# Loads of k, r and v that wait for the landing of the load two ahead

## The chip, the cores and the metric

The kernel runs on one core of a Trainium2 chip. The metric is device time in microseconds; the lower, the better. The kernel before took 514.64 us, the median of nine runs (513.17 to 515.85).

## What is computed

Two steps follow each other. The first is a recurrence over 768 positions, for 4 batches and 8 heads of 48 channels, in float32:

```python
for t in range(S):
    kt, vt, rt = (k[:, :, t], v[:, :, t], r[:, :, t])
    cur = np.einsum('bhd,bhe->bhde', u[None] * kt, vt)
    y[:, :, t] = np.einsum('bhd,bhde->bhe', rt, state + cur)
    state = w[None, :, :, None] * state + np.einsum('bhd,bhe->bhde', kt, vt)
```

The second is a multiplicative feed-forward net on the 3072 rows of 384 channels which that gives:

```python
a = x @ w1
b = x @ w2
h = a * b @ w3
return (h @ w_out)
```

The weights w1, w2 (384 x 1024), w3 (1024 x 1024) and w_out (1024 x 384) come as float64.

## The kernel before

**The recurrence** is cut into 24 units: 6 chunks of 128 positions (`NCH`), times 4 batches. A unit `n` needs its k and r (in `krin[n % 3]`) and its v (in `vnat[n % 3]`). Each of these three is one DMA of 192 KB, 128 positions by 8 heads by 48 channels, which `load` issues on SP's queue (L197 to L204). In memory a position of one head is a run of 48 numbers, so such a load consists of 1024 runs of 192 bytes.

DVE then scales k and r (`scale`, L392) and forms the products for the diagonal (`rk`, L401; `rku`, L404; `dots`, L408). PE turns k and r (L439) and ACT copies them back (L446, L449). For later units DVE turns blocks itself (`turn_blocks`, L461), SP writes them to a scratch in HBM (`turn_out`, L465) and reads them back in four pieces (`turn_places`, L473), and ACT copies the keys out (`turn_rows`, L478). PE forms the products of the recurrence: `adds` (L505, needs v and the scaled k), `products` (L512, needs the turned k and r), `with_state` (L612, needs the state that ACT spread out in L537), `with_pairs` (L626, needs v). ACT takes the result out as `xT` (`take`, L634).

**The weights** come in 32 pieces, also on SP's queue (`fetch`, L218 to L223): 8 of 768 KB (w1 and w2), 8 of 384 KB (w_out), 16 of 512 KB (w3), into three buffers in turn. Each float64 word is made into a float32 in five steps, two on ACT (`magnitude` L342, `low` L354) and three on DVE (`sign` L347, `high` L350, `total` L357). w3 and w_out are multiplied into one matrix first (`fold`, L370 to L383).

**The net** then runs by chunk: `product_ab` (L652) on PE makes a or b for 128 of the 1024 channels, three matmul steps over 384 channels, into one of two PSUM buffers (`psF`). `take_a` (L658) on ACT copies a out and so frees its buffer, `multiply` (L663) on DVE multiplies b by it and frees the other. The product with the folded matrix is done in seven half-size products (`product` L709, `gather`, `store` L742).

**What sets the order.** For the decay values of this input, the arm with a list of instructions written out by hand is taken: `ORDER` (L22 to L88), whose words are run one after the other by `listed` (L745 to L756). Under `manual_schedule` each of PE, ACT, DVE and SP does its instructions in the order of that list. `kr.4` is the load of k and r of unit 4, `v.4` that of v, `W.4` the fetch of weight piece 4, `y.5` and `z.5` the scratch write and its four reads, `l.11` the ACT copy after them, `M.3` the first ACT step of weight piece 3, `a.1.5.2`, `c.1.5.2`, `b.1.5.2`, `u.1.5.2` are `product_ab` of a, `take_a`, `product_ab` of b and `multiply` for chunk 1, channel block 5. All DMAs of the kernel are issued by SP, in that one order. What stands ahead of the list (the loads of units 0 and 1, weight pieces 0 and 1, w and u, L227 to L237) is placed by the scheduler. The DMAs use eight completion semaphores in turn, so that a DMA is not issued before the eighth one ahead of it has landed.

Of the kernel before, what the change touches and what calls it, by code (L numbers as in the profile page):

```python
# [14 lines left out]
COPY = mybir.ActivationFunctionType.Copy  # L15
ABS = mybir.ActivationFunctionType.Abs
PSUM = bass.MemoryType.PSUM
PE, ACT, DVE, SP = (getattr(mybir.EngineType, x) for x in ("PE", "Activation", "DVE", "SP"))


# [64 lines left out]
u.5.7.2 s.5.3.0 P.5.0.1 s.5.3.2 E.5.1.0 s.5.3.1 s.5.3.3 P.5.0.2 E.5.0.1 P.5.0.3 E.5.0.2 P.5.0.4 E.5.0.3 P.5.0.5  # L85
E.5.0.4 P.5.0.6 E.5.0.6 E.5.0.5 D.5.0.0 P.5.1.2 E.5.0.7 D.5.0.1 P.5.1.1 E.5.1.2 P.5.1.3 E.5.1.1 P.5.1.4 E.5.1.3
P.5.1.5 E.5.1.4 P.5.1.6 E.5.1.6 E.5.1.5 D.5.1.0 E.5.1.7 D.5.1.1
"""  # L88


@with_exitstack
def kernel(
# [34 lines left out]
    nc = tc.nc  # L127
# [66 lines left out]
    units = [(c, b) for c in range(NCH) for b in range(B)]  # L194
    NU = len(units)

    def load(n, which="krv"):  # L197
        if n >= NU:
            return
        c, b = units[n]  # L200
        ts = slice(c * C, (c + 1) * C)
        for nm, src, dst in (("k", k, krin[n % NIN][:, 0]), ("r", r, krin[n % NIN][:, 1]), ("v", v, vnat[n % NV][:, :, :D])):
            if nm in which:
                nc.sync.dma_start(out=dst, in_=src[b, :, ts, :].rearrange("h t d -> t h d"))  # L204

    w1 = const.tile([P, DF // STRIP, KM, STRIP], F32)
    w2 = const.tile([P, DF // STRIP, KM, STRIP], F32)
# [6 lines left out]
    pieces = [src for src, _ in strips] + [moe_w_out[j * P:(j + 1) * P, None, :] for j in range(KF)] \  # L214
        + [moe_w3[j * P:(j + 1) * P, None, z * PIECE:(z + 1) * PIECE] for j in range(KF) for z in range(NW3)]
    landed = {}
# [11 lines left out]
    for i in range(2):  # L228
        nc.sync.dma_start(out=wucol[i * PAD:i * PAD + D], in_=w.rearrange("(p i) (d o) -> i d p o", i=2, o=1)[i])
    load(0, "kr")  # L230
    fetch(0)
    nc.sync.dma_start(out=ub.rearrange("t h d -> t (h d)"),
                      in_=u.rearrange("h d -> (h d)").rearrange("(o n) -> o n", o=1).to_broadcast([P, DM]))
    load(0, "v")
    load(1, "kr")
    fetch(1)
    load(1, "v")  # L237
# [10 lines left out]
    pn_in = const.tile([C, 2, H, PAD], F32)  # L248
    with tc.tile_pool(name="once", bufs=1) as once, tc.tile_pool(name="psW", bufs=2, space=PSUM) as psW:

# [29 lines left out]
    def program(fast):  # L280
        with ExitStack() as arm:
            body(arm, fast)

    def body(arm, fast):
# [4 lines left out]
        once = fold_pool.enter_context(tc.tile_pool(name="fold", bufs=1))  # L289
        psT = arm.enter_context(tc.tile_pool(name="psT", bufs=2, space=PSUM))  # L290
        psA = arm.enter_context(tc.tile_pool(name="psA", bufs=1, space=PSUM))
        psY = arm.enter_context(tc.tile_pool(name="psY", bufs=1, space=PSUM))
        psF = arm.enter_context(tc.tile_pool(name="psF", bufs=2, space=PSUM))

# [532 lines left out]
            seven(NCH - 2)  # L827
            seven(NCH - 1)

        at_start = dict(landed)  # L830
        (listed if fast else plain)()
        landed.clear()
        landed.update(at_start)

# [34 lines left out]
```

## Time and profile before

| | |
|---|---|
| median of nine runs | 514.64 us (513.17 to 515.85) |
| the profiled execution: its own time | 514.53 us |
| its span, first instruction to last | 512.7 us |
| PE busy (matmul) | 489.8 us, 96% of the span |
| DVE busy | 278.2 us, 54% |
| ACT busy | 183.1 us, 36% |
| moved by DMA | 52.72 MB; 77729 of 96865 packets under 512 B |
| loads of k, r, v: number, median from issue to landing | 24 each; 3.9, 4.4, 4.1 us |
| weight pieces of 768, 512, 384 KB: the same | 8, 16, 8; 6.2, 5.1, 3.6 us |
| mean granted TensorE clock | 0.996 |

All times of the profile are of one execution. A line of the page or the timeline gives start and length, engine, source line, what is written and read, and in brackets how long the engine stood idle before it and what ended that. "SPq" is the issue of a DMA: its length is the time that SP spends in issuing, not that of the transfer. The landing of a transfer is told apart from it, as the time from issue to landing. "issue" as the cause of idle time means that the engine waited for nothing that the profile shows.

### The profile page before, as it was taken

The page shows a single profiled execution, that of the slowest core. Times are in us where ns is not written, and L with a number is a line of the kernel's source. Part 1 is how long each engine was busy: PE and PEld are TensorE (multiplying, and loading weights), DVE is VectorE, ACT ScalarE, POOL GpSimd, SP SyncE. Part 2 cuts the span into 40 slices and gives each one's busy share as a digit, 9 for nine tenths or more (in the row PEclk, how much of TensorE's full clock was granted, in tenths as well). Part 3 has the DMA queues.
Part 4 walks back from the last instruction along what each step waited for, and adds up shares of the span by engine and source line. Part 5 has one row for each costly group of instructions (what it writes and reads, how often), then busy time and mean ns, then how long its engine had stood idle before and what let it go on. Part 6 is the DMA issues. An engine that isn't in the chain of part 4 may idle for free.

```text
span 512.7 us, 12195 instructions
## 1 busy us (share of the span) xinstructions
PE 489.8 (96%) x5192; PEld 320.9 (63%) x5192; DVE 278.2 (54%) x587; ACT 183.1 (36%) x455; POOL 6.0 (1%) x23
## 2 busy tenths in 40 slices
PE   1789999999999999999999999999999999999996
PEld 1667555455466666678887487564965654855486
DVE  6978998888386866756325432285322215221442
ACT  3767556666377754403103200341061410001000
POOL 4000000000000000000000000000000000000000
PEclk9989999999999999999999999999999999999999
DMA  7998797768549770304402201230050100000001
GB/s 170 232 249 221 184 246 194 190 226 238 148 118 224 191 205 15 78 1 101 132 32 77 64 0 46 64 110 2 1 163 9 49 1 0 17 15 17 1 17 67
DMA packets 96865, 52.72 MB, mean 103 GB/s; under 512 B 77729, under 2 KB 88226, under 8 KB 96802
## 3 DMA queue, kind: packets, MB, share of 16 engines
q1 hardware_dynamic: 96802, 51.86, 37.5%
q8 instruction: 43, 0.70, 0.6%
q14 instruction: 20, 0.16, 0.1%
HBM read 39.65 MB, written 12.19 MB: 101 GB/s over the span
## 4 chain that ended last, share of the span: by engine, by line
PE 86%; DMA 6%; DVE 4%; issue 2%; ACT 1%; SPq 1%; DVEq 0%; ACTq 0%
PE ps_a L652 22%; PE ps_b L652 22%; PE ps_w L380 8%; PE ps_y L612 3%; PE ps_s4b L709 3%; PE ps_a12b L709 3%; PE ps_a22t L709 3%; PE ps_s2t L709 3%; PE ps_s3t L709 3%; PE ps_s1t L709 3%; PE ps_y L626 3%; PE ps_a11b L709 3%; PE ps_a L512 2%; DMA tt<-scratch 2%; PE ps_a L505 2%
## 5 line engine op out<-in xcount | busy, mean ns | idle before, releaser
L652 PE MATMUL ps_a<-xT,w 128*128 128x512 f32 (+1 forms) x300 | 132.5, 585 | 0.0
L652 PE MATMUL ps_b<-xT,w 128*128 128x512 f32 (+1 forms) x300 | 131.0, 578 | 0.0
L652 PEld LDWEIGHTS ps_b<-xT,w 128*128 128x128 f32 x300 | 56.0, 190 | 62.4 <-issue 56.9
L663 DVE TENSOR_TENSOR abt<-ps_b,a 128x512 f32<-128x512 f32 (+1 forms) x50 | 33.4, 667 | 110.4 <-PE ps_b L652 110.4
L652 PEld LDWEIGHTS ps_a<-xT,w 128*128 128x128 f32 x300 | 56.1, 193 | 57.1 <-issue 53.5
L658 ACT COPY a<-ps_a 128x512 f32<-128x512 f32 (+1 forms) x50 | 28.1, 565 | 130.2 <-PE ps_a L652 126.4
L537 ACT COPY wide<-st 64x192 f32<-64x192 f32 x88 | 30.6, 348 | 58.9 <-DVE st L529 28.1
L380 PE MATMUL ps_w<-wo,w3T 128*128 128x384 f32 x128 | 42.5, 487 | 0.0
L419 ACT ACTIVATE AT<-same,dg 128x64 f32<-128x64 f32 x160 | 40.4, 336 | 5.4 <-DVE dg L408 2.9
L380 PEld LDWEIGHTS ps_w<-wo,w3T 128*128 128x128 f32 x128 | 23.9, 190 | 15.7 <-ACT wide L537 0.2
L354 ACT ACTIVATE t<-raw 128x512 uint32<-128x512 uint32 (+2 forms) x32 | 22.4, 706 | 7.8 <-DVE w3n L350 5.0
L626 PE MATMUL ps_y<-AT,vnat 64*64 64x64 f32 x1152 | 22.7, 222 | 0.6 <-issue 0.6
L392 DVE TENSOR_TENSOR krs<-krin,pn_in 128x768 f32<-128x768 f32 x24 | 22.8, 950 | 0.5 <-PE ps_a L505 0.4
L540 DVE COPY_PREDICATED AT<-later,ps_a 128x512 f32<-128x512 int32 x24 | 17.5, 730 | 9.5 <-PE ps_a L505 5.8
L612 PEld LDWEIGHTS ps_y<-tt,wide 128*32 128x32 f32 x1056 | 15.9, 110 | 10.6 <-issue 6.3
L505 PE MATMUL ps_a<-vnat,krs 64*64 64x48 f32 x704 | 16.8, 224 | 5.6 <-DVE krs L392 3.3
L626 PEld LDWEIGHTS ps_y<-AT,vnat 64*64 64x64 f32 x1152 | 19.3, 134 | 3.9 <-issue 2.0
L612 PE MATMUL ps_y<-tt,wide 128*32 128x64 f32 x1056 | 19.7, 221 | 1.7 <-ACT xT L634 1.7
L461 DVE STREAM_TRANSPOSE tr<-krs 128x768 f32<-128x768 f32 x19 | 18.5, 974 | 5.1 <-DMA scratch<-tr 5.0
L505 PEld LDWEIGHTS ps_a<-vnat,krs 64*64 64x64 f32 x704 | 14.3, 139 | 9.7 <-issue 9.2
L512 PEld LDWEIGHTS ps_a<-tt,kT 64*64 64x64 f32 x768 | 14.4, 136 | 7.6 <-issue 3.5
L528 DVE TENSOR_TENSOR st<-ps_a,st 128x192 f32<-128x192 f32 x40 | 14.0, 349 | 8.1 <-PE ps_a L505 4.8
(102 smaller groups left out, 560.4 us busy)
## 6 DMA issues: line engine op xcount, KB each, us to landing
raw<-in_moe_w_dram SPq DMA_DIRECT2D x16, 512.0 KB, 5.1
scratch<-tr SPq DMA_DIRECT2D x19, 384.0 KB, 3.7
raw<-in_moe_w_dram SPq DMA_DIRECT2D x8, 768.0 KB, 6.2
tt<-scratch SPq DMA_DIRECT2D x38, 128.0 KB, 3.1
krin<-in_k_dram SPq DMA_DIRECT2D x24, 192.0 KB, 3.9
krin<-in_r_dram SPq DMA_DIRECT2D x24, 192.0 KB, 4.4
vnat<-in_v_dram SPq DMA_DIRECT2D x24, 192.0 KB, 4.1
raw<-in_moe_w_out_dram SPq DMA_DIRECT2D x8, 384.0 KB, 3.6
```

The lines of the kernel that those rows point to most:

```text
L380: nc.tensor.matmul(ps, lhsT=w3T[j][:, kc, :], rhs=wo[kc], start=(kc == 0), stop=(kc == KF - 1))
L392: nc.vector.tensor_mul(krs[n % NS][:, :, :, :D], kr, pn[:, :, :, :D])
L419: nc.scalar.activation(out=AT[n][:, i, p, :], in_=same, func=COPY, scale=dg[n][:, h:h + 1])
L505: nc.tensor.matmul(added(n)[rows(i), a, p, :], lhsT=kk[rows(a), 2 * p + i, :], rhs=vnat[n % NV][rows(a), 2 * p + i, 0:D], start=True, stop ...
L512: nc.tensor.matmul(upper(n)[rows(a), i, p, :], lhsT=kT[n][rows(i), p, rows(a)], rhs=rT[n][rows(i), p, 2 * a:2 * a + 2], start=True, stop=True)
L537: nc.scalar.copy(out=wide[a][n % 2][rows(i), :, i * D:(i + 1) * D], in_=st[units[n][1]][rows(i)])
L612: nc.tensor.matmul(yt[n][g * Q:(g + 1) * Q, a, q, :], lhsT=wide[a][n % 2][:, p, j * Q:(j + 1) * Q], rhs=rw[:, p, 2 * a:2 * a + 2] if fast ...
L626: nc.tensor.matmul(yt[n][rows(g), a, q, :], lhsT=vv[rows(a), x:x + PAD], rhs=AT[n][rows(a), h % 2, h // 2, :], start=(a, g) not in seen, s ...
L652: nc.tensor.matmul(ps, lhsT=(w1 if x == "a" else w2)[:, z, q, js], rhs=xT[c][:, q, ts], start=(q == 0), stop=(q == KM - 1))
L658: nc.scalar.copy(out=a, in_=ps)
L663: nc.vector.tensor_mul(abt[c, j][:, parts_of_tokens[part]], factor["b", c, j, part], factor["sa", c, j, part])
L709: nc.tensor.matmul(ps, lhsT=of[:, m * C:(m + 1) * C], rhs=w34[:, KH * (x == 1) + j, :DH] if x < 2 else made[b][:, j, :], start=(j == 0), s ...
```

## The change

Every load of k, r or v, from the third on, gets a dependence on the load of k, r or v two ahead of it in the order of the program: it is issued only when that one has landed. Weights, scratch writes and reads, and the stores of the output get none. A list `small` keeps the loads, and is set back for the second arm of the program.

```diff
+ONE_AFTER_THE_OTHER = mybir.DependencyInfo(mybir.DependencyClass.Sync, mybir.DependencyReason.DATA)
...
+    small = []
+
     def load(n, which="krv"):
+
         if n >= NU:
             return
...
             if nm in which:
-                nc.sync.dma_start(out=dst, in_=src[b, :, ts, :].rearrange("h t d -> t h d"))
+                small.append(nc.sync.dma_start(out=dst, in_=src[b, :, ts, :].rearrange("h t d -> t h d")))
+                if len(small) > 2:
+                    tc.add_manual_dep(small[-1].ins, small[-3].ins.name, ONE_AFTER_THE_OTHER, reason="few small pieces at a time")
...
-        at_start = dict(landed)
+        at_start, small_at_start = dict(landed), list(small)
         (listed if fast else plain)()
+        small[:] = small_at_start
         landed.clear()
         landed.update(at_start)
```

## The prediction

> **What bounds the kernel now.** I read the page's slices first, then the chain of waits in order of time, the timeline of the start, and last the landing of single transfers.
>
> ```profile
> PE   1789999999999999999999999999999999999996
> DVE  6978998888386866756325432285322215221442
> ACT  3767556666377754403103200341061410001000
> DMA  7998797768549770304402201230050100000001
> ```
>
> Each digit is a tenth of 12.8 us. From the fourth slice to the end PE is the bound. Before that it waits: of its 22.9 us of idle time (span 512.7, busy 489.8) most lies in the first three slices, where DMA and DVE are both nearly full. So a delay before about 31 us moves all that PE has left to do, and later one moves it only where PE stands next to a wait. The chain of the start:
>
> ```profile
> 17.59 6.45 DMA krin<-in_r_dram
> ...
> 24.16 0.13 DVE ruk L401
> ...
> 27.64 0.66 PE ps_rT L439 x4
> 28.30 0.25 PE ps_a L505 x5
> 28.55 2.10 issue
> 30.64 0.82 PE ps_a L505 x27
> ```
>
> Columns: start, length, what. The load of r for unit 3 lands at 24.04 and DVE's `rk(3)` follows at once: a load is on the path, with no slack (DVE idle 0.40 us there). The 2.10 us of "issue" stand between equal matmuls, where no wait can be.
>
> ```profile
> 5.80 4.03 SPq L204 DMA_DIRECT2D krin<-in_r_dram  x1
> 16.17 0.84 SPq L223 DMA_DIRECT2D raw<-in_moe_w_dram  x1
> 22.40 0.93 ACT L342 ACTIVATE w<-raw 128x768 f32<-128x768 f32 x1 [0.98 <-DMA raw<-in_moe_w_dram]
> 25.39 0.54 PE L612 MATMUL ps_y<-tt,wide 128*32 128x64 f32 x24 [1.74 <-ACT xT L634]
> ```
>
> First line: the third small load in a row behind a weight stands 4.03 us in its issue. So the queue already takes no more than about three of them. Last two: weight piece 2 (landed 22.38) is awaited by ACT, whose list is `high word, low word, wide, xT`, and PE's `with_state(1)` waits for that xT.
>
> **What the Trainium skill says.** "DMA: Bandwidth & Descriptors", section "Queues, rings and completion order": on each DMA engine descriptors are consumed in ring order, and the engine takes its queues in turn. The trace agrees in effect: all loads of the start land in the order of issue (r of unit 0 at 5.8, the weight at 9.4, u at 10.0, v at 10.7). A load issued later can therefore not overtake, and one held back finds what was put ahead of it. Section "Anatomy of one DMA": a wait for a semaphore is done by the issuing sequencer, before the DMA, and about 2 us of a DMA are fixed. Here 192 KB alone take 2.8 us to landing and follow each other at 0.7 us when queued, so 2.1 us are fixed. "Runtime: NRT & Kernel Launch", section "Instruction fetch mechanics": instructions come by DMA in blocks of 16 KiB, 256 of them. The page has 43 instruction packets, 0.70 MB, which is 16 KB each; one starts at 28.2, and PE goes on at 30.64. I take the 2.10 us of "issue" for that fetch.
>
> **The change.** It adds no DMA and removes none; the listed order of PE, DVE, ACT and SP is the same in the built program. Each load of k, r or v (72 of 192 KB) waits on SP for the landing of the one two ahead. SP is in order, so weights, scratch and tt transfers behind it wait too. One thing moves: ahead of the listed part, weight 1 is now issued before r of unit 1. The wait instruction itself is 17 ns (the semaphore rows of L204), nothing here.
>
> ```profile
> L204 SPq DMA_DIRECT2D vnat<-in_v_dram x1: 396/396/396, 142.8 to 142.8; - x1
> DMA to landing us min/median/max: 2.8/2.8/2.8
> ```
>
> This one is alone; in a full queue the v issued at 15.43 took 4.3. Two in flight that must land first, at 2.8 to 4.3 us a round, are a load per 1.4 to 2.1 us, against 0.7 queued. I take 3.2 us for a fresh load (k at 81.92: 3.0; r at 127.85: 3.6), or 0.7 after the landing before it, whichever is later. For a 768 KB weight: 5.7 (median 6.2, that at 9.87: 5.7) or 2.5 after the landing before it (3.3 and 2.2 seen).
>
> *Start, replayed on SP.* Unit 0 as before: k 5.1, r 5.8, weight 0 9.4, u 10.0. v0 waits for k0, issued 5.2, lands 10.7 as before. k1 (waits r0) 11.4. Weight 1, not held, issued 6.45, lands 11.4+2.5=13.9 (15.6 before). r1 waits for v0, issued 10.75, lands 13.9+0.7=14.6 (12.26). v1 11.45, lands 15.3. k2 waits for r1: 14.65, 17.85. r2 waits for v1: 15.35, 18.55. v2 waits for k2: 17.9, 21.1. Weight 2 behind it: issued 18.35 (16.17 before), lands 24.05 (22.38). k3 24.75. r3 waits for v2: issued 21.15, behind weight 2 and k3, lands 25.45 (24.04). Weight 3: issued after r4 at 26.1, lands 31.8 (29.02).
>
> What this does: `rk(1)` on DVE from 13.35 to 14.65, `rk(3)` from 24.16 to 25.5, so DVE is 1.35 late at `scale(3)`. ACT starts weight 2 1.65 late, and with it xT of unit 0 and PE's `with_state(1)`. PE reaches `adds(2)` 1.35 to 1.65 late, and the fetch, started by the matmuls ahead of it, is as late: I take **1.5 us**. With 3.0 us a load it is 0.7 to 1.0 (r3 at 25.1), with 4.3 it is 4 (r3 at 28.1). Early weight 1 brings nothing: ACT takes it at 17.09 after other work. Late weight 3 is hidden: ACT's three steps behind it end at 34.2, before take_a at 34.85+1.5. v3 lands at about 36, needed at 38.4; the scratch of unit 5 goes out some 3 us late, its ACT copy then about 1.5 us late of its shifted place, before take_a copies that have 0.7 and 2.0 us of idle time, and products(5) has 6.5 us of slack.
>
> *Later.* Of the 49 loads after 46 us most find the landing two ahead long over. Issue by issue, 14 of them have to wait, up to 4.9 us (r16 at 155), and nearly all have slack, since k and r are used 4 to 80 us after landing. Where something with a deadline is queued behind:
>
> ```profile
> 127.85 0.81 SPq L204 DMA_DIRECT2D krin<-in_r_dram  x1
> 128.76 0.89 SPq L465 DMA_DIRECT2D scratch<-tr  x1
> 137.88 0.62 ACT L478 COPY kT<-tt 128x512 f32<-128x512 f32 x1 [3.15 <-DMA tt<-scratch]
> 138.40 0.58 ACT L658 COPY a<-ps_a 128x512 f32<-128x512 f32 x1
> 139.09 2.78 PE L652 MATMUL ps_b<-xT,w 128*128 128x512 f32 x6
> ```
>
> r14 must wait for v11 (issued 126.75, landed 129.7): 1.9 us late. Behind it the scratch of unit 11 goes from 128.76 to 130.45, lands 3.6 later at 134.1 (132.4), and the four tt reads wait for that landing. ACT stands idle 3.15 us for them with take_a of (1,6) queued behind, and PE starts b of (1,5) 0.1 us after that copy ends. There is no cover. If the scratch sets the reads' landing, PE loses 1.7; if weight 26, which shares the queue until 137.0, sets it, 0.3. I take **1.0**. Unit 13 has the same pattern (r16, scratch at 158.99, about 1.7 late at the tt copy), but 1.02 us of slack at `products(13)` and a fetch gap of 0.65 us inside it: 0 to 0.8, taken as 0. Sum: 1.5+1.0=2.5 us.
>
> **Rivals.** (1) *No change, 514.5.* The issue of the third small load was blocked anyhow, and the new wait takes the place of that block. For it: blocked issues of 3 to 4 us at 5.8, 12.3, 19.2, 30.3. Against: a blocked load is already queued and lands 0.7 after its neighbour, a waiting one pays the 2.1 fixed us again; and r3 has no slack. (2) *Faster, 513.0.* With less queued, instruction blocks reach PE sooner. The stalls of this kind are 2.10 at 28.6, 0.60 at 43.8 and 0.65 at 170.2, together 3.35; if the loads' delay is hidden by half (+0.8) and the stalls shrink by 2.3, it is 514.5-1.5=513.0. It decides once the stall before 30.64 shrinks by more than the start is late. For it: DMA is 97 to 98% busy there. Against: engines take queues in turn, so the length of one queue should matter little to the other. (3) *Slower by more, 519.7.* A fresh load takes 4.3 us also in the thinner queue, as the v at 15.43 did: about 3.5 at the start (r3 4 late, the mean of DVE and ACT a little less) and 1.7 at unit 11, 514.5+5.2=519.7. Against: that v was issued when DMA was full, which the change itself ends.
>
> **How the numbers follow.** The profiled execution took 514.53 us (span 512.7, 1.8 around it), the median of nine is 514.64, so the sum is made on 514.5: 514.5+2.5=**517.0 us**. Chances: this 0.57, (1) 0.2, (2) 0.15, (3) 0.08. The low end lies under (1) at 514.0, leaving out (2); the high end at 519.5 takes in the 4 of the start with the middle of the later term and leaves out the upper part of (3). A change within 0.2% (1.03 us) can't be told from none; slower by more is the forecast and (3): 0.65, within 0.2, faster 0.15.
>
> **What would show it.** Issues of L204 no longer than about 1 us, landing in 3 to 4 us where they were 5 to 6.5; r3 at 25 to 26 and weight 2 at about 24; PE's first `a` product at 33.8 instead of 32.3; DMA under 9 in the second and third slices; ACT's tt copy of unit 11 about 2.5 late. It is wrong if r3 lands by 24.5, if the "issue" stall of 2.10 us is gone, or if PE makes up a late start between 31 and 130 us.

## The result

The changed kernel took 519.94 us (median of 10 runs, 517.65 to 523.49), the kernel before 515.03 in the runs beside it. The ratio is 1.0097, with a 95% interval of 1.0074 to 1.012: slower by 5.0 us (3.8 to 6.2). The prediction said slower, by 2.5 us. So the direction was right, the mechanism in the main, and the size was half of what came.

In what follows a ratio is always that to the kernel before on the same chip, and 0.001 of it is 0.51 us. The times of one kernel spread over 4 to 9 us, and a profile shows one of them. Seven of the kernels below (the changed one, e1, e6, e10, e11, e14, e16) are the same program up to 45 us, and in their traces PE is at 44 us between 0.9 us ahead of the kernel before and 1.9 behind it. So a shift of under about 3 us between two profiles proves little by itself; the medians decide, and what many traces have in common.

### The profile after

The lines of the code stand seven lower than before from `load` on (L505 is L512, L612 is L619). The profiled execution took 519.69 us, with a span of 517.9. First the page's slices, each a fortieth of the span:

```profile
PE   1769999999999899999999999999999999999996
DMA  7788787769637592201701301220041100000001
```

DMA has lost the nines of slices 2 and 3, as predicted. How much, the windows say: length, busy time of each engine, clock, DMA share and GB/s from 12 to 40 us, for the kernel before and then for the changed one.

```profile
12.00:40.00 28.00, 21.67 (x495) 17.79 (x496) 23.94 (x43) 19.75 (x46) 0.00 (x0) 0.94 0.97 245
```

```profile
12.00:40.00 28.00, 19.59 (x442) 16.54 (x443) 22.02 (x40) 18.75 (x43) 0.00 (x0) 0.94 0.78 194
```

The share falls from 0.97 to 0.78 and the rate from 245 to 194 GB/s, in a stage in which PE, DVE and ACT wait for what DMA brings. This is the number to remember from the profile after. The loads themselves are about as many: 14 are issued in this window before and 13 after. What is missing is weights: weights 5 and 6 go out at 33.86 and 36.19 before, and at 40.12 and 40.70 after. Two pieces of 768 KB in 28 us are 56 GB/s (an estimate), as much as the difference. Next the timeline of the start, in which the issue of r of unit 1, the issue of weight 2, ACT's first step on it and PE's `with_state(1)` answer to the lines shown of before:

```profile
10.76 0.37 SPq L209 DMA_DIRECT2D krin<-in_r_dram  x1
18.82 0.58 SPq L230 DMA_DIRECT2D raw<-in_moe_w_dram  x1
24.91 0.90 ACT L349 ACTIVATE w<-raw 128x768 f32<-128x768 f32 x1 [1.74 <-DMA raw<-in_moe_w_dram]
27.85 0.87 PE L619 MATMUL ps_y<-tt,wide 128*32 128x64 f32 x24 [2.78 <-ACT xT L641]
38.98 0.68 PE L512 MATMUL ps_a<-vnat,krs 64*64 64x48 f32 x32 [2.62 <-DMA vnat<-in_v_dram]
```

The blocked issue of 4.03 us is gone: this one took 0.37. But weight 2 goes out at 18.82 instead of 16.17, ACT takes it at 24.91 instead of 22.40, and `with_state(1)` comes at 27.85 instead of 25.39. The last line is new: PE stands 2.62 us ahead of `adds(3)` for v of unit 3. Then three pieces of the chain that ended last (start, length, what), the landings of weights 2, 4 and 5:

```profile
18.82 6.07 DMA raw<-in_moe_w_dram
30.94 7.25 DMA raw<-in_moe_w_dram
40.12 5.91 DMA raw<-in_moe_w_dram
```

DMA holds 16% of the chain now (6% before), and up to 46 us most of the chain is landings of loads and weights. The 2.10 us of "issue" at 28.55 that the chain of before had are not in it any more: that stall is gone, and so is one of 0.60 us at 44.38. Last the places of the scratch copies, at unit 5, unit 11 and unit 13:

```profile
58.52 0.62 ACT L485 COPY kT<-tt 128x512 f32<-128x512 f32 x1 [5.30 <-DMA tt<-scratch]
...
141.44 0.62 ACT L485 COPY kT<-tt 128x512 f32<-128x512 f32 x1 [2.86 <-DMA tt<-scratch]
142.94 2.74 PE L659 MATMUL ps_b<-xT,w 128*128 128x512 f32 x6
...
174.41 0.62 ACT L485 COPY kT<-tt 128x512 f32<-128x512 f32 x1 [3.92 <-DMA tt<-scratch]
175.08 0.52 PE L519 MATMUL ps_a<-tt,kT 64*64 64x64 f32 x13 [0.85 <-ACT kT L485]
```

At unit 11, where the prediction put 1.0 us, PE starts b with no idle time. At unit 13, where it put nothing, PE stands 0.85 us for the copy. The same copy of unit 13 in the kernel before:

```profile
168.03 0.62 ACT L478 COPY kT<-tt 128x512 f32<-128x512 f32 x1 [1.85 <-DMA tt<-scratch]
169.68 0.53 PE L512 MATMUL ps_a<-tt,kT 64*64 64x64 f32 x13
```

It comes 6.4 us later in the changed kernel, where PE is 4.4 us late by then.

The shift of the same PE instruction, after less before, gives the course (worked out from the two traces): +1.5 us at 15.75, +3.4 at 27, then only +0.4 at 32 (the stall is gone), +2.0 at `adds(3)`, +1.3 at 44, +3.1 at 57 (unit 5's scratch), +3.9 at 75, no change up to 145, +5.4 at 172, +6.1 at 178, +5.4 at the end.

### The profile page after: what moved, and what is told of

Same layout as the page of the kernel before. It is cut to its first block, busy times and chain, and to the rows that moved or that the text cites. A ratio compares the mean times of both kernels' runs of the same rounds, so it can differ in the third digit from the quotient of the medians.

```text
span 517.9 us, 12199 instructions
## 1 busy us (share of the span) xinstructions
PE 491.1 (95%) x5192; PEld 321.7 (62%) x5192; DVE 278.2 (54%) x587; ACT 182.8 (35%) x455; POOL 6.0 (1%) x23
## 4 chain that ended last, share of the span: by engine, by line
PE 73%; DMA 16%; ACT 5%; DVE 3%; SPq 2%; issue 1%; ACTq 0%; DVEq 0%
PE ps_a L659 20%; PE ps_b L659 18%; DMA raw<-in_moe_w_dram 7%; PE ps_w L387 6%; PE ps_s4b L716 3%; PE ps_a22t L716 3%; PE ps_a12b L716 3%; PE ps_s2t L716 3%; PE ps_s1t L716 3%; PE ps_s3t L716 3%; PE ps_a11b L716 3%; DMA raw<-in_moe_w_out_dram 3%; DMA tt<-scratch 2%; PE ps_y L619 2%; PE ps_a L519 2%; PE ps_y L633 2%
## 5 line engine op out<-in xcount | busy, mean ns | idle before, releaser
L619 PEld LDWEIGHTS ps_y<-tt,wide 128*32 128x32 f32 x1056 | 16.7, 112 | 13.1 <-issue 7.5
L619 PE MATMUL ps_y<-tt,wide 128*32 128x64 f32 x1056 | 21.4, 226 | 3.6 <-ACT xT L641 2.8
L512 PE MATMUL ps_a<-vnat,krs 64*64 64x48 f32 x704 | 16.3, 223 | 6.1 <-DVE krs L399 3.3
L485 ACT COPY kT<-tt 128x512 f32<-128x512 f32 x19 | 11.7, 618 | 25.2 <-DMA tt<-scratch 22.1
L512 PEld LDWEIGHTS ps_a<-vnat,krs 64*64 64x64 f32 x704 | 14.0, 138 | 10.2 <-issue 9.5
```

The costliest lines, as they stand in the source:

```text
L512: nc.tensor.matmul(added(n)[rows(i), a, p, :], lhsT=kk[rows(a), 2 * p + i, :], rhs=vnat[n % NV][rows(a), 2 * p + i, 0:D], start=True, stop ...
L619: nc.tensor.matmul(yt[n][g * Q:(g + 1) * Q, a, q, :], lhsT=wide[a][n % 2][:, p, j * Q:(j + 1) * Q], rhs=rw[:, p, 2 * a:2 * a + 2] if fast ...
```

## The experiments

### Which half of the waits costs

Four variants of the condition in `load`; the rest is the changed kernel.

```diff
-                if len(small) > 2:
+                if 2 < len(small) < 24:      # e1: loads up to v of unit 6
+                if len(small) > 23:          # e2: loads after that
-                    tc.add_manual_dep(small[-1].ins, small[-3].ins.name, ...)
+                    tc.add_manual_dep(small[-1].ins, small[-4].ins.name, ...)   # e3: three ahead (if len(small) > 3)
+                    tc.add_manual_dep(small[-1].ins, small[-2].ins.name, ...)   # e4: one ahead (if len(small) > 1)
```

> Edit: only the loads up to v of unit 6 (issued before about 50 us) wait for the landing two ahead, the later 49 do not. Theory A (most of the cost arises at the start, where weights, v of unit 3 and the scratch of unit 5 queue behind waiting loads; in the two traces PE is 3.8 us late by 70 us): 3.5 to 4 us over the kernel before, about 518.5. Rival B (the cost arises later, at units 13 and 14, and the start is made up by the instruction fetch that no longer stalls): within 1 us of the kernel before. Rival C (every wait costs its share, 20 of 34 real waits are early): about 3 us.

Measured: 1.004 (1.0024 to 1.0055), +2.1 us.

> Edit: only the loads after v of unit 6 wait, those of the first 50 us do not. Theory A: 1.5 us over the kernel before (units 13 and 14 in the trace: 0.5, 1.1 and 0.6 minus 0.6), about 516. Rival B: 4 to 5 us over. Rival C: about 2 us. PE's shift should begin at about 160 us, at products of unit 12 or 13, and not at unit 11, whose scratch was late in the changed kernel's trace without cost.

Measured: 1.0043 (1.0023 to 1.0063), +2.2 us.

> Edit: each load waits for the landing of the one three ahead, so three may be in flight. Theory A: the queue of before took no more than about three of them beside a weight, so this comes near to what the blocked issue did: 0 to 1 us over the kernel before. Rival D (what costs is that a load is issued only after a landing, and pays the fixed 2 us again, however many are in flight): half of the change's cost or more, 2.5 to 4 us.

Measured: 0.999 (0.9968 to 1.0011), no difference.

> Edit: each load waits for the landing of the one just ahead, one in flight. Theory A: 22 loads of the start at 3.2 us each and 6 weights of 2.5 between them make about 85 us where the kernel before has 46; v of unit 3 comes at about 60 instead of 37, so 20 to 28 us over the kernel before, about 538. If the waits were mostly covered by DVE and ACT work (rival B), under 10 us.

Measured: 1.0936 (1.0895 to 1.0977), +48 us.

The two halves cost about the same and make 4.3 of the 5.0 us. So the early waits cost less than theory A had it, and the late ones more. One ahead costs twice what A expected, two ahead 5 us, three ahead nothing: the cost is that of too few loads in flight. A wait as such cost nothing that shows: with three ahead at least 10 loads went out only when the awaited one had landed, 8 of them in the first 46 us (24 and 15 with two ahead). The rate of one ahead in the same window:

```profile
12.00:40.00 28.00, 14.93 (x328) 12.41 (x328) 15.35 (x27) 12.33 (x31) 0.00 (x0) 0.91 0.43 96
```

96 GB/s, against 194 with two ahead. With three ahead the trace has 237, with none 245.

The traces also show what the early waits give back. PE's timeline around `adds(2)`, with the waits only late (e2):

```profile
27.91 0.32 PE L512 MATMUL ps_a<-vnat,krs 64*64 64x48 f32 x5
30.32 0.92 PE L512 MATMUL ps_a<-vnat,krs 64*64 64x48 f32 x27 [2.10 <-issue]
```

and with the waits only early (e1):

```profile
29.62 0.68 PE L512 MATMUL ps_a<-vnat,krs 64*64 64x48 f32 x32
38.00 0.68 PE L512 MATMUL ps_a<-vnat,krs 64*64 64x48 f32 x32 [2.28 <-DMA vnat<-in_v_dram]
```

In the first the 32 matmuls of `adds(2)` are cut after five by a stall of 2.10 us, in the second they run through. So the first half of rival 2 was right. Its price is the last line: the v of unit 3 comes too late, and what was won is lost there. This is not chance of one trace: in all seven kernels that are the same up to 45 us PE stands 1.1 to 2.6 us ahead of `adds(3)`, and in the kernels whose early loads are free or wait for three ahead it does not stand there.

### The late half: scratch writes behind waiting loads

In `ORDER` the scratch write of a unit is put ahead of the loads that stand before it on SP's queue. e6 moves three of them in the changed kernel, e9 is the same order in the kernel before, e10 and e11 take e6 apart. The words of `ORDER` that move:

```diff
-v.5 r.4 x.5 ... y.5
+r.4 x.5 ... y.5 v.5                        # unit 5: e6, e9, e10, e14
-kr.16 Q.25 ... y.13 ... kr.17 A.12 ... v.14 g.13 ... y.14
+Q.25 ... y.13 kr.16 ... A.12 ... g.13 ... y.14 kr.17 v.14   # units 13, 14: e6, e9, e11
```

> The changed kernel with all its waits, but the scratch write of unit 5 is issued ahead of v of unit 5, that of unit 13 ahead of k and r of unit 16, and that of unit 14 ahead of k and r of unit 17 and v of unit 14. Theory A (the late half of the cost is scratch writes that stand behind waiting loads, at units 13 and 14; that of unit 5 costs another 1 us in the early half): it takes back 1.1 us at unit 5 and 1.1 to 1.7 us at units 13 and 14; 517.0 to 518.0. Rival B (the late half is spread over many small delays): 519 to 520.

Measured: 1.0007 (0.9982 to 1.0031), 515.5 us: 4.6 of the 5.0 us are gone.

> The kernel before, without waits, with the same three scratch writes (units 5, 13, 14) issued ahead of the loads: the control for the run that had this order with the waits (4.4 us below the changed kernel). Theory A (the scratch writes stand behind waiting loads, and without waits they lose next to nothing by standing there): 514 to 515.5 beside the kernel before at 515, so that the whole 4.4 us belong to the waits. Rival F (the scratch writes are late in the kernel before as well, and the order is worth as much there): 511 to 512.5, so that the waits still cost about 4 us in the new order too.

Measured: 0.999 (0.9965 to 1.0014), no difference. The interval leaves the order by itself 1.8 us of gain at most, so most of the 4.6 us that e6 took back belonged to the waits.

> The changed kernel with all its waits, only the scratch write of unit 5 issued ahead of v of unit 5. Theory A: its share of the 4.4 us by the gaps in the traces is half, 2.0 us: 517.5 to 518.5 beside the changed kernel's 519.9. Rival: what it gains is lost at the next wait, 519.5 or more.

Measured: 1.0125 (1.0081 to 1.0169; six runs), nothing gained.

> The changed kernel with all its waits, only the scratch writes of units 13 and 14 issued ahead of k and r of unit 16, k and r of unit 17 and v of unit 14. Theory A: this is the whole late half of the cost, 2.2 us: 517.3 to 518.3. Rival: the moved loads collide with the reads of scratch behind them, 519.5 or more.

Measured: 1.0041 (1.0022 to 1.006): 2.9 us less than the whole change.

So the late half lies at units 13 and 14, in scratch transfers behind waiting loads. How it comes about is seen on SP's timeline. First the kernel before, then the changed one:

```profile
154.10 0.38 SPq L204 DMA_DIRECT2D vnat<-in_v_dram  x1
155.21 3.67 SPq L204 DMA_DIRECT2D krin<-in_r_dram  x1
158.99 0.85 SPq L465 DMA_DIRECT2D scratch<-tr  x1
162.23 1.08 SPq L204 DMA_DIRECT2D vnat<-in_v_dram  x1
163.53 1.89 SPq L473 DMA_DIRECT2D tt<-scratch  x4
```

```profile
157.95 0.38 SPq L209 DMA_DIRECT2D vnat<-in_v_dram  x1
158.37 1.12 SPq L209 DMA_DIRECT2D krin<-in_k_dram  x1
163.97 0.37 SPq L209 DMA_DIRECT2D krin<-in_r_dram  x1
164.44 1.52 SPq L472 DMA_DIRECT2D scratch<-tr  x1
169.33 0.37 SPq L209 DMA_DIRECT2D vnat<-in_v_dram  x1
169.79 1.94 SPq L480 DMA_DIRECT2D tt<-scratch  x4
```

v of unit 13 is issued behind two weight pieces and lands at 163.91. r of unit 16 waits for it from 159.5 to 163.97, though it is needed only at 170, and the scratch write stands behind r. In the kernel before the same r stood 3.67 us in its issue, so the write leaves only 1.6 us later when counted from the issue of v of unit 13 (6.49 us after it, 4.89 before). A second wait comes on top. The write lands at 168.20, but v of unit 14, which waits for k of unit 17, stands ahead of the four reads until 169.33: the reads go out 1.6 us after the landing of the write, where in the kernel before they followed it at once (163.51, 163.53). In e11 neither is held up:

```profile
160.86 0.33 SPq L472 DMA_DIRECT2D scratch<-tr  x1
161.23 0.43 SPq L209 DMA_DIRECT2D krin<-in_k_dram  x1
164.60 2.17 SPq L480 DMA_DIRECT2D tt<-scratch  x4
```

The write leaves at 160.86, ACT's copy comes at 170.03 instead of 174.41, and `products(13)` starts at 173.50 without idle time instead of 175.08.

Not all of the 2.9 us need belong to the waits. PE stops inside `products(13)` for an "issue" of 0.4 to 1.2 us in twelve of the 20 traces (0.65 in the kernel before and in the changed one), and in none of the seven in which the scratch write of unit 13 goes first, e8 and e9 without waits among them. So this order also takes that stall away.

e10 shows how a lead can be lost again. By its trace PE is 3.4 us ahead of the changed kernel at 57 us (2.0 of them at 44 us already, where the two are still the same program), and 1.3 ahead at 101. In between, ACT waits for a w_out piece that was issued 2.5 us earlier than in the changed kernel and landed only 1.3 earlier:

```profile
99.00 0.56 ACT L349 ACTIVATE wo<-raw 128x384 f32<-128x384 f32 x1 [2.54 <-DMA raw<-in_moe_w_out_dram]
100.52 1.98 PE L659 MATMUL ps_b<-xT,w 128*128 128x512 f32 x4 [1.83 <-ACT a L665]
```

e16 moves the scratch of unit 11 as well (`v.11 kr.14` behind `y.11`).

> The whole change with its waits, and the scratch writes of units 5, 11, 13 and 14 ahead of the loads: the run with units 5, 13 and 14 gave 515.5. Theory A (the wait predicted at unit 11 is there as soon as what came before it is faster): 513.5 to 514.8, and no wait of PE at b of unit 11's time. Rival (it came from other transfers): 515 to 516.

Measured: 1.0031 (1.001 to 1.0053), not better than e6. PE still stands at b of unit 11's time:

```profile
138.48 0.62 ACT L485 COPY kT<-tt 128x512 f32<-128x512 f32 x1 [4.51 <-DMA tt<-scratch]
139.64 1.55 PE L659 MATMUL ps_b<-xT,w 128*128 128x512 f32 x3 [1.14 <-ACT a L665]
```

The write left early, at 126.64, but its reads then stood behind r of unit 14, which waited, and behind weight 26: they were issued only at 132.77. So PE can stand at unit 11: 1.58, 1.53 and 1.14 us in e6, e11 and e16. But a waiting r of unit 14 ahead of the write is not enough for it. In e2 and e13, where the write stands behind it too and PE comes 0.9 us earlier and 1.2 us later than in the kernel before, PE starts b without idle time, as in the changed kernel. In e6 and e11 the transfers of this stretch took longer: v of unit 11 landed after 4.74 and 4.97 us and the scratch write after 4.95 and 4.97, against 2.98 and 3.29 in the changed kernel, though e11 is the same program up to there. What slowed them is open. Whether unit 11's waits keep anything back in e6 by the medians, these runs do not tell.

### The early half: no single load

Each of these takes a suspect off. e5 puts weights 2 to 4 and v of unit 3 ahead of loads that wait:

```diff
-kr.2 v.2 d.0 W.2 ... e.1 kr.4 ... T.1 W.3 ... R.2 kr.5 ... W.4 Q.1 v.3
+kr.2 W.2 v.2 d.0 ... e.1 W.3 kr.4 ... T.1 ... R.2 ... W.4 Q.1 v.3 kr.5
```

> The changed kernel with all its waits, but in the order of SP's queue weight 2 is issued ahead of v of unit 2, weight 3 ahead of k of unit 4, and weight 4 and v of unit 3 ahead of k of unit 5, so that they no longer stand behind loads that wait. Theory A (the early cost is the late landing of weight 2 ahead of unit 1's with_state, and of v of unit 3 ahead of adds(3)): it takes back 2 to 2.5 us at weight 2 and 1.5 to 2 us at v of unit 3, of which the two can overlap; 516 to 517.5 beside the changed kernel's 519.9. Rival B (the loads themselves, k and r of units 1 to 5, come too late for VectorE): nothing is gained, or the moved loads come later still, 519.5 to 521.

Measured: 1.0126 (1.009 to 1.0162; six runs), nothing gained.

e13 begins the waits with unit 2 (`if len(small) > 6`), so that the start ahead of the list is as it was.

> The changed kernel, but its waits begin with k of unit 2: r and v of unit 1 are issued as before, and weight 1 isn't moved ahead of r of unit 1. Theory A (the start term as predicted, 1.46 us at 15.75 us in the trace, is lost in the wait for weight 2 and v of unit 3 that follow, which the loads from unit 2 on set anyway): 519 to 520, like the whole change. Rival H (the start term goes through to the end as I predicted): 518 to 518.7, 1.5 us below the whole change.

Measured: 1.0092 (1.006 to 1.0123), like the whole change, within 2 us.

e14 is e1 with the scratch of unit 5 ahead of v of unit 5, e15 is e1 with `v.3` ahead of `W.4`.

> The waits on the loads up to v of unit 6 only, and the scratch write of unit 5 ahead of v of unit 5. Beside the early waits alone (516.3, 2.1 us above before). Theory A (scratch of unit 5 is most of the early half): 514.3 to 515. Rival I (v of unit 3 is): 516 to 516.5, no gain.

Measured: 1.0033 (1.0012 to 1.0053; one of the 22 times is 1777 us, which no theory here explains and which does not move the median), beside 1.004 for e1 no difference that can be told.

> The waits on the loads up to v of unit 6 only, and v of unit 3 issued ahead of weight 4, which is needed later. Rival I (v of unit 3, landing behind weight 4, is the early half): 514 to 515, the PE wait of 2.3 to 2.6 us ahead of adds(3) gone. Theory A (scratch of unit 5): 516 to 516.5.

Measured: 1.0072 (1.005 to 1.0094), slower than e1.

No suspect taken off brought a gain that shows, and the traces say in what way. In e15 PE no longer waits for v of unit 3, and waits for weight 4 instead, which now stands behind it:

```profile
39.88 0.90 ACT L349 ACTIVATE w<-raw 128x768 f32<-128x768 f32 x1 [3.15 <-DMA raw<-in_moe_w_dram]
42.32 0.66 PE L446 MATMUL ps_kT<-ident,krs 128*128 128x128 f32 x4 [3.17 <-ACT kT L453]
```

In e13 weight 2 lands at 24.12, as late as in the seven kernels that are the same up to 45 us (24.07 to 24.89; 22.38 before), and PE, which is not late at 15.75 now, stands longer ahead of `with_state(1)`:

```profile
27.06 0.54 PE L619 MATMUL ps_y<-tt,wide 128*32 128x64 f32 x24 [3.56 <-ACT xT L641]
```

In e5 the r of unit 3 is late, since the v of unit 2 that it waits for stands behind weight 2; DVE stands 2.85 us for it (in e7, the same program up to there, that load came 1.8 us earlier). A cost that moves to the next transfer whenever one is taken out of its way looks like one of throughput. Weight 5 shows it best: on SP's queue it stands behind v of unit 4, so it goes out when the 19 loads ahead of it have. In the eleven kernels whose early loads wait for the one two ahead it goes out at 37.8 to 41.1 us, whatever the order and the start (38.29 in e13, 39.64 in e5). Where they are free or wait for three ahead it goes out at 33.9 to 35.5 (31.85 in e12, which leaves four loads out), and with one ahead at 58.54. Then the two orders together (e5's and e6's) were measured with two in flight (e7), with none held (e8), and with three in flight (e18); e17 is e5's order with none held.

> The changed kernel with all its waits and both of these changes of order. Theory A: the costs add up and so do their removals; with the prompt instruction fetch kept (the 2 us stall ahead of adds(2) gone) it comes out at 512.5 to 515, level with the kernel before or up to 2 us faster. Rival B: 518 to 520. Rival C (the instruction fetch waits again as soon as weights are issued early, so the stall returns): 515 to 517.

Measured: 1.0044 (1.0018 to 1.007).

> The kernel before, without waits, in the same changed order as the run with both changes: the control for what the order does by itself. Theory A: without waits nothing stood behind a waiting load, so the order is worth little: 513 to 515, with the instruction fetch stall of about 2 us still ahead of adds(2). Rival: the order alone brings the weights so much earlier that it gains 2 us or more: under 512.5.

Measured: 0.9936 (0.9912 to 0.9961), 3.3 us faster than the kernel before.

> The kernel before, without waits, with weights 2, 3 and 4 and v of unit 3 issued ahead as in the run with the waits (520.7). The order with both moves and no waits gave 510.8, that with only the scratch writes moved 515.0. Theory J (all of that gain is the weights' order; the waits undo it because the loads' rate then holds back weights 5 and 6): 510.5 to 512. Rival: 514 to 515.5, the gain of both comes from their combination.

Measured: 0.997 (0.9952 to 0.9988), 1.5 us faster.

> Both moves of order, and each load waits for the one three ahead of it instead of two. Theory J (two in flight are too few for the first 45 us, three are enough, as they were in the order before): 510.5 to 512.5, level with the same order without waits. Rival (in the better order any wait in front of weights 5 and 6 costs): 514 to 517.

Measured: 0.9944 (0.9925 to 0.9962), 2.9 us faster: level with e8, and 5.1 us under e7. In the same order, then, two in flight cost 5.6 us and three nothing that can be measured. The window from 12 to 40 us in e18:

```profile
12.00:40.00 28.00, 22.66 (x558) 18.80 (x559) 25.09 (x44) 21.78 (x51) 0.00 (x0) 1.00 0.98 254
```

254 GB/s. What the lack of rate costs in e7 is seen at weight 5, which SP issues at 41.07 there and at 34.42 in e18:

```profile
47.37 0.91 ACT L349 ACTIVATE w<-raw 128x768 f32<-128x768 f32 x1 [5.89 <-DMA raw<-in_moe_w_dram]
48.70 2.60 PE L659 MATMUL ps_a<-xT,w 128*128 128x256 f32 x6 [4.15 <-ACT xT L641]
```

e8, e18 and, by less, e17 beat both kernels, and the waits have no part in it: e8 and e17 have none. The weights' order makes about half of the gain of e8 and e18 (e17). The scratch writes, which by themselves gave nothing that shows (e9), may make the rest, by the stall inside `products(13)` for one thing; the intervals of e8 and e17 overlap.

### The instruction stall

e12 leaves out the loads of k and r of units 4 and 5 in the kernel before (`kr.4` and `kr.5` struck from `ORDER`).

> The kernel before, without waits, with the loads of k and r of units 4 and 5 left out (units 4 and 5 then work on the k and r of units 1 and 2): fewer bytes are queued when the second 16 KB block of instructions is asked for, at about 25 us. Theory E (a full queue of loads delays the fetch of instructions by 3 to 5 us, and the waits of the changed kernel made it prompt): the second fetch starts within 1.5 us of the point where it starts at once in the changed kernel, beside 4.8 us in the kernel before, the stall of 2.10 us ahead of adds(2) shrinks to under 1 us, and 511.5 to 513.5 comes out. Rival G (the stall belongs to the place in the program and not to the load on the queues): the stall of 2 us stays, 514 to 515.5.

Measured: 1.0004 (0.998 to 1.0028), and the stall stayed:

```profile
31.75 0.67 PE L505 MATMUL ps_a<-vnat,krs 64*64 64x48 f32 x27 [1.84 <-issue]
```

Theory E failed in the form in which it was put: 768 KB less in loads did not make the fetch prompt. That the stall is a fetch is seen in all traces together. PE stops with "issue" for 0.3 us or more 28 times in the listed part. In 27 of them (not in one of e4) the place is one of five PE instructions, and PE goes on 1.3 to 1.6 us after a 16 KB instruction packet has ended. When the packet comes differs from group to group. Take as zero the PE instruction at which the earliest of them starts the second 16 KB instruction packet of the listed part. Where the early loads wait for the one or two ahead, the packet starts 0.0 to 1.3 us after it (eleven kernels; 2.9 in e7, which is the same program as e5, with 1.3, up to there). Where they are free or wait for three ahead, it starts 3.8 to 6.0 us after it (before, e2, e3, e8, e9, e12, e17, e18). The stall inside `adds(2)` follows: 0.7 to 3.5 us in the second group, none in the first but for 0.6 in e7. In e12 the queue is still filled without limit, only with other transfers, which fits; but what in the queue holds the packet up was not found.

## Why the prediction was right in sign and wrong in size

**The mechanism held.** A load that waits pays its fixed time again (with one in flight, in e4, the loads from 12 to 40 us took 2.5 to 3.4 us each, one after the other), and transfers with a deadline stand behind it. Most issues of L209 took 0.37 to 0.40 us and none over 1.51, where up to 4.03 had been needed, k and r landed after 3.2 and 3.5 us (median), and DMA fell under nine tenths in the second and third slices. The Trainium skill's statement that was used for it ("DMA: Bandwidth & Descriptors", "Anatomy of one DMA — SWDGE (gpsimd) path": the wait is done by the sequencer that issues, before the DMA, and about 2 us of one are fixed) gives its 2 us for DMAs that GpSimd issues, while SP issues these; the prediction's 2.1 us from its own trace is what counts here. The ladder of one, two and three in flight, 96, 194 and 237 GB/s, fits it. The prediction also concluded that a load issued later cannot overtake. The section it named for this, "Queues, rings and completion order", does not say so: of two descriptors taken in order "a later one may finish its write before an earlier one". What carries the conclusion is the traces: in none of the 20 does a recorded landing come ahead of that of a DMA issued earlier. What the prediction did not do is to work out the pace of the loads for the whole stage; it replayed loads one by one up to unit 3 and called the rest hidden.

**The sum, term by term.** The prediction had 1.5 us at the start, 1.0 at unit 11 and 0 at unit 13. The runs have 2.1 (e1), nothing that shows in the changed kernel, and 2.9 at units 13 and 14 (e11). So the step that failed most is the one that put unit 13 at nothing.

**Start, 1.5 us predicted.** Measured by itself 2.1 (e1), so the size is near, but the parts were not. The replay was right for k and r within a microsecond: r1 15.5 (14.6), weight 2 24.9 (24.05), r3 26.1 (25.45). It took 3.2 us for a fresh load and 5.7 for a weight; the loads issued from 12 to 40 us took 4.0 (median of the 11 with a landing on record; 2.7 to 5.1), and weights 2 to 5 took 5.4 to 7.3, so the error grew. In this the step failed:

- "and the fetch ... is as late": the stall of 2.10 us did not move, it vanished. Rival 2 named this, and the prediction itself called it a sign of being wrong; it was set aside because the engines take queues in turn, and the traces speak against that reason. Without the gift the start would have cost about 4 us (an estimate, 2.1 of e1 and 2.1 of the stall).
- "v3 lands at about 36, needed at 38.4": it landed at 38.84, behind a weight 4 that took 7.25 us, and PE stood 2.62 us.
- "Late weight 3 is hidden" held (PE starts its first a at 32.69 without idle time), but there is no word of weights 4 to 6: weight 5 went out at 40.12 instead of 33.86, and PE stood 0.44 us for ACT's work behind it, 4.15 in e7.

That the first 1.46 us at 15.75 lead to the end, as the step had it, is not borne out: with them gone (e13) PE comes to `adds(3)` at 37.32, and in the seven kernels with all early waits at 36.87 to 38.98 (median 37.53). The medians of e13 and the changed kernel can't decide it; their difference is 0.3 us, give or take 2.

**Unit 11, 1.0 us predicted, none measured in the changed kernel.** The step had two cases, 1.7 us if the scratch write sets the landing of the reads and 0.3 if weight 26 does, and took the middle. The second came. The copy follows the issue of v of unit 11 by 11.36 us, against 11.13 before, and the reads land 0.6 to 1.4 us after weight 26 (0.4 to 0.8 before). v of unit 11 itself went out 3.3 us late, as PE was 3.8 late. The first case shows in e6 and e11, where the write landed late enough.

**Unit 13, taken as 0: the term that was mis-sized.** It cost, with unit 14, 2.9 us (e11; the interval of the difference is about 1.4 to 4.3). The trace has 1.05 us of it at `products(13)`, where the step gave 0 to 0.8, and 0.7 at the `with_state` behind the scratch of unit 14, at which the step did not look. The step had the scratch write about right, 1.7 us late (1.6). What it left out is v of unit 14, which waits for k of unit 17 and holds the reads of that scratch up for another 1.6. So the copy came 6.4 us later than before, 2.0 more than PE was late by then, with 1.02 of slack. How much of the 2.9 is the stall that the order of e11 also took away stays open.

**Scratch of unit 5, said to be hidden.** By the trace of the changed kernel it cost PE 1.9 us. Taking it out gave nothing beside the late waits (e10) nor beside the early ones alone (e14), but e6, which has it, is 1.7 us under e11, which has not. What it is worth in the median stays open.

**The rivals.** No change (1) is out. Faster (2) was right in its mechanism and short in its balance: it gave back about 2 us of about 7 (an estimate, the 5.0 measured and the 2.1 of the stall). Slower by more (3), 519.7, hit the number, by luck in part: it put 3.5 us at the start and 1.7 at unit 11, with r of unit 3 4 us late (2.1) by a load of 4.3 us. Over the whole kernel k and r took 3.2 and 3.5, but from 12 to 40 us the loads took 4.0, nearer to its 4.3 than to the 3.2 that the prediction took.

## What to carry to other kernels

A limit on how many loads are in flight sets the pace of everything that stands behind them on the queue. Before replaying single transfers, count how many loads must go ahead of the last transfer that the stage needs (here 19 ahead of weight 5), and at what pace they can. When each removed wait brings up the next one, stop looking for the culprit and measure the rate. On a queue that is served in order, put what has a deadline (here a scratch write and its reads) ahead of what may wait, or a load that nobody needs yet will hold it up.

## What the runs showed that was not expected

The second instruction packet of the listed part comes 4 to 6 us after its earliest point when the loads are issued without limit or with three in flight, and at most 1.3 us after it (2.9 in e7) when only one or two of the 192 KB loads are in flight; that was worth a stall of 0.7 to 3.5 us in one place. A like stall of 0.4 to 1.2 us at `products(13)` went away by moving a scratch write, with waits and without. In an order with the weights ahead, the first stall was still there (e8 1.55 us, e18 1.27 us), and these are nevertheless the fastest kernels: beside e7, the same order with two in flight, the pace of the loads was worth more than the prompt fetch.
